# Batch 0 of an FFT-filtered gated FFN: both exchanges between transform stages moved from DRAM onto the chip

## The chip, the core and the metric

The kernel runs on one core of a Trainium2 chip. A core has five engines that work from queues of their own: TensorE (PE: matmuls; PEld: its weight loads), VectorE (DVE), ScalarE (ACT), GpSimd (POOL) and SyncE (SP, which only issues DMA transfers here). The metric is device time in microseconds (us), the median over runs. The profile is of one further execution.

## The reference

Eight sequences x of 3136 tokens by 256 channels are filtered along the tokens in the frequency domain, and then go through a gated feed-forward network with 1024 hidden channels.

```python
X = np.fft.rfft(x, axis=1)
Y = X * (filt_r + 1j * filt_i)[None]
x = np.fft.irfft(Y, n=3136, axis=1)
h = np.maximum(x @ w_in, 0.0)
conv_out = ...  # depthwise, 3 taps along the tokens, weights conv_w
out = (h * (1.0 / (1.0 + np.exp(-conv_out)))) @ w_out
```

Inputs x and filt are float32; w_in, conv_w and w_out arrive as float64 and are turned into float32 on the chip.

## The kernel before

**The transform.** 3136 is 112 times 28. One sequence goes through four matmul stages, each in 14 steps ("pairs" q, two of 28 columns each):

- Stage 1: for a pair of residues n, a matmul over 112 tokens gives 112 numbers (2 parts s, real and imaginary, 28 groups g) for 256 channels. `by_column` (L229) makes it with the table as the stationary operand: numbers on partitions, channels in the free dimension.
- Stage 2: for a pair of groups g, a matmul over (n, r), which is 28 times 4 rows, gives 56 bins in two layouts; `filt` (L240) multiplies by the filter on DVE (L244 to L246) and adds on POOL (L247).
- Stage 3: `by_column` again, with the inverse tables (in_i) and z from `filt`.
- Stage 4: `fourth` (L250): here the data is the stationary operand and a table the moving one, so the outcome has channels on partitions, as the network needs it. It is split into a rounded part (`hi_act` on ACT, L145) and a rest (`lo_dve` on DVE, L148), both called y.

Between stages 1 and 2, and between 3 and 4, the rows have to be regrouped: what lay on 112 partitions for one n is wanted as (n, r) rows for one g. Before the change this goes through DRAM: `store` (L224) copies PSUM to st on ACT (L226) and writes a_dram or b_dram, and loads (`load_in`, L219) read them back with another view.

**The order of the work.** Batch 0's transform and the weight conversion stand in a block of their own at the start (L262 to L388), written out by hand in the order of every engine's queue. After it comes the main loop (L575 on), in which the network of batch t-1 and the transform of batch t run together by a plan; its first matmuls over y (L176 to L178, tile ps_h) need all of batch 0's y for the first tokens, hence all 14 steps of stage 4.

The block before, in order: SP loads stage 1's tables (tab from in_s) and x (rows), the conv weights and the first weight chunks (raw); stage 1 runs and its stores go out on ACT's DMA queue; SP loads the filters (f), the inverse tables, and the rows of a_dram; stages 2 and 3 run interleaved, step i of stage 2 beside step i-3 of stage 3; four steps of batch 1's stage 1 follow (AHEAD); SP loads the rows of b_dram; stage 4 runs.

**The weight conversion.** `to_f32` (L153) turns one chunk of float64 into float32 with seven DVE instructions (L159 to L171) and one POOL add (L173); there are eight chunks of 128x512 and a small one ("c", the conv weights). `split_weights` (L289) splits a chunk into rounded part and rest: two ACT copies, two POOL subtractions. Chunk buffers (raw) are three, so the load of chunk k+3 waits for the conversion that held the buffer. Before, chunks c and 0 to 2 are converted ahead of stage 2, then 3 to 5, and 6 and 7 within stages 2 and 3.

**The filters.** f has four buffers. For each pair two DMAs load one half each into 64 partitions (L304, L305), and ACT copies them to the other 56 partitions (L309, L310).

Of the kernel before, what the change touches and what calls it, by code (L numbers as in the profile page):

```python
# [17 lines left out]
N1 = 112  # L18
# [20 lines left out]
def _dft_tables():  # L39
# [69 lines left out]
    return {"s1": s1, "s2": s2(False), "s2s": s2(True), "i1": i1, "m2": m2}  # L109
# [15 lines left out]
def tile_fft_filter_gated_ffn(  # L125
# [10 lines left out]
    s2s: bass.AP,  # L136
    i1: bass.AP,
# [54 lines left out]
    s2s_sb = wc.tile([112, 120], F32, name="s2s_sb")  # L192
    cw = wc.tile([128, 3, NF], F32, name="cw")
# [9 lines left out]
    yps = [ctx.enter_context(tc.tile_pool(name="y_even", bufs=1, side="right"))]  # L203
# [46 lines left out]
    def fourth(ps, br):  # L250

        for j in range(2):
            for k in range(KT):
                o = ps[:, (2 * k + j) * N1:(2 * k + j + 1) * N1]
                nc.tensor.matmul(o, lhsT=br[:, j, 128 * k:128 * k + 128], rhs=m2_sb, start=True, stop=True)  # L255
# [6 lines left out]
    with (  # L262
        tc.tile_pool(name="sp", bufs=2) as sp,
# [3 lines left out]
        raws, fts, tabs, rows, zs = {}, {}, {}, {}, {}  # L267

        def load_weights(k):
            raws[k] = raw = sp.tile([128, 2, 512], I32, name="raw", bufs=3)  # L270
            for part, src in enumerate((w_in, w_out)):
                nc.sync.dma_start(out=raw[:, part], in_=src[:, 512 * k:512 * k + 512])

        def load_conv():
            raws["c"] = raw = sp.tile([128, 2, 512], I32, name="raw", bufs=3)
            nc.sync.dma_start(out=raw[:, 0, 0:6 * NF], in_=conv_w)

        def convert(k):

            raw = raws.pop(k)  # L280
            em = sp.tile([128, 2, 512], I32, name="em")
# [3 lines left out]
            else:  # L285
                ws[k] = w = sp.tile([128, 2, 256], F32, name="ws", bufs=8)
                yield from to_f32(w.rearrange("p t n -> p (t n)"), raw.rearrange("p t n -> p (t n)"), em[:, 0], em[:, 1])

# [8 lines left out]
        def table(kind, c):  # L297
            k, src, n = {"1": (112, s1, 7), "3": (120, i1, 3)}[kind]
            tabs[kind, c] = t = sp.tile([120, 4, 112], F32, name=f"tab{kind}", bufs=n)[0:k]
            nc.sync.dma_start(out=t, in_=src[:, 4 * c:4 * c + 4])  # L300

        def load_filter(q):
            fts[q] = f = sp.tile([120, 2, 2, D], F32, name="f", bufs=4)
            nc.sync.dma_start(out=f[0:64, :, 0], in_=filt_in[0:64, pair(q), 0])  # L304
            nc.sync.dma_start(out=f[56:120, :, 1], in_=filt_in[56:120, pair(q), 1])  # L305

        def copy_filter(q):
            f = fts[q]
            nc.scalar.activation(f[64:120, :, 0], f[0:56, :, 0], AF.Copy)  # L309
            nc.scalar.activation(f[0:56, :, 1], f[64:120, :, 1], AF.Copy)  # L310
            if q == NP - 1:
                nc.scalar.dma_start(out=f[92:93, 1, 0], in_=nyq)

        def load(kind, b, q):
            rows[kind, q] = load_in(sp, kind, b, q, 12, "rows")

        def column_stage(kind, b, q, r):
            ps = sps.tile([128, 512], F32, name="ps")
            by_column(ps, tabs[kind, q // 2][:, 2 * (q % 2):2 * (q % 2) + 2], r)
            store(tp, kind, b, q, ps, 3, "st", nc.scalar)  # L320

        ws = {}
        for c in range(7):
            table("1", c)
            load("1", 0, 2 * c)
            load("1", 0, 2 * c + 1)
            if c == 0:
                load_conv()
            if c < 2:
                load_weights(c)  # L330
        for dst, src in ((s2_sb, s2[:, 0:120]), (s2s_sb, s2s[:, 0:120]), (m2_sb, m2)):
            nc.sync.dma_start(out=dst, in_=src)
        for k in ("c", 0, 1, 2):
            for _ in convert(k):
                pass
            load_weights(2 if k == "c" else k + 3)
        for q in range(NP):
            column_stage("1", 0, q, rows.pop(("1", q)))
        for q in range(4):
            load_filter(q)  # L340
        for c in range(2):
            table("3", c)
        for q in range(NP):
            load("2", 0, q)
        for k in (3, 4, 5):
            for _ in convert(k):
                pass
            if k + 3 < 8:
                load_weights(k + 3)
        table("3", 2)  # L350
        for q in range(4):
            copy_filter(q)
        late = (x for k in (6, 7) for x in convert(k))
        pss = {}
        for i in range(NP + 4):
            if i < NP:
                pss[i] = ps = sps.tile([128, 512], F32, name="ps")
                second(ps, i, rows.pop(("2", i)))
            if 0 <= i - 3 < NP:
                q = i - 3  # L360
                column_stage("3", 0, q, zs.pop(q))
                if q % 2 and q // 2 + 3 < 7:
                    table("3", q // 2 + 3)
            if 0 <= i - 1 < NP:
                zs[i - 1] = filt(pss.pop(i - 1), i - 1, fts.pop(i - 1))
# [289 lines left out]
```

## Time and profile before

| | |
|---|---|
| median of 3 runs | 1602.9 us (1602.11 to 1603.8) |
| the profiled execution, its own time | 1603.2 us |
| its span in the trace | 1601.4 us |
| mean granted TensorE clock | 0.982 |
| PE matmul busy | 1525.1 us (95%) |
| DVE, ACT, POOL busy | 1197.2, 1202.3, 874.8 us |
| DMA, mean over the span | 149 GB/s, 238.32 MB |
| first matmul that waits for batch 0's y | starts at 130.93 us |

The profile has one line for a group of instructions, with the source line, the engine, output and inputs by the program's names, the shape, the count, the busy time and the mean duration. A timeline line begins with the start and the duration in us; in brackets stands how long the engine had been idle and what ended that. "Issue" is waiting that no recorded event explains. An ordinary float32 matmul appears as two MATMUL records (the 56 matmuls of stage 4 are 112 records). "Granted clock" is the share of full speed that TensorE was allowed.

### The profile page before, as it was taken

The page shows a single profiled execution, that of the slowest core. Times are in us where ns is not written, and L with a number is a line of the kernel's source. Part 1 is how long each engine was busy: PE and PEld are TensorE (multiplying, and loading weights), DVE is VectorE, ACT ScalarE, POOL GpSimd, SP SyncE. Part 2 cuts the span into 40 slices and gives each one's busy share as a digit, 9 for nine tenths or more (in the row PEclk, how much of TensorE's full clock was granted, in tenths as well). Part 3 has the DMA queues.
Part 4 walks back from the last instruction along what each step waited for, and adds up shares of the span by engine and source line. Part 5 has one row for each costly group of instructions (what it writes and reads, how often), then busy time and mean ns, then how long its engine had stood idle before and what let it go on. Part 6 is the DMA issues. An engine that isn't in the chain of part 4 may idle for free.

```text
span 1601.4 us, 28391 instructions
## 1 busy us (share of the span) xinstructions
PE 1525.1 (95%) x9424; PEld 1366.8 (85%) x9424; DVE 1197.2 (75%) x1966; ACT 1202.3 (75%) x2623; POOL 874.8 (55%) x1170
## 2 busy tenths in 40 slices
PE   4569999999999999999999999999999999999999
PEld 3248889988899888998899987998889988899998
DVE  4856887578866787768876778767887788777876
ACT  2448667876699767986678866887669966799897
POOL 1452555655566455655556555565556755576554
PEclk8679999999999999999999999999999999999999
DMA  9876565465544665356553565546554445320001
GB/s 298 242 213 199 178 187 165 144 190 155 166 128 145 182 185 152 111 158 188 163 165 110 167 180 150 152 129 183 158 164 131 134 129 175 101 66 24 24 24 37
DMA packets 171874, 238.32 MB, mean 149 GB/s; under 512 B 16744, under 2 KB 119505, under 8 KB 171729
## 3 DMA queue, kind: packets, MB, share of 16 engines
q1 hardware_dynamic: 165615, 229.17, 48.1%
q10 hardware_dynamic: 6114, 7.34, 1.4%
q8 instruction: 75, 1.23, 0.3%
q14 instruction: 70, 0.57, 0.1%
HBM read 159.38 MB, written 77.07 MB: 148 GB/s over the span
## 4 chain that ended last, share of the span: by engine, by line
PE 62%; issue 14%; POOL 9%; DVE 6%; DMA 3%; ACT 3%; SPq 1%; POOLq 0%; ACTq 0%; DVEq 0%
PE po L459 8%; PE po L460 8%; PE po L461 8%; PE ps_h L176 8%; PE ps_h L177 8%; PE ps_h L178 8%; PE ps_t L231 7%; POOL g L151 6%; PE ps_t L255 5%; DVE t L423 2%; POOL gm L151 2%; PE ps_t L235 2%; ACT t L419 1%; POOL z L247 1%; DMA raw<-in_w_out 1%
## 5 line engine op out<-in xcount | busy, mean ns | idle before, releaser
L423 DVE SCALAR_TENSOR_TENSOR t<-ps_h,cw,t 128x448 f32<-128x448 f32 x896 | 608.0, 679 | 329.7 <-ACT t L419 324.9
L151 POOL TENSOR_TENSOR g<-t,g 128x384 fp32r<-128x384 f32 x448 | 455.2, 1016 | 200.8 <-ACT g L145 88.2
L419 ACT ACTIVATE t<-ps_h,cw 128x448 f32<-128x448 f32 x448 | 284.5, 635 | 241.2 <-POOL gm L151 209.1
L176 PE MATMUL ps_h<-y,wi 128*128 128x450 f32 x896 | 410.2, 458 | 0.0
L459 PE MATMUL po<-wo,g 128*128 128x256 f32 x1344 | 374.2, 278 | 0.5
L460 PE MATMUL po<-wo,g 128*128 128x256 f32 x1344 | 373.9, 278 | 0.0
L461 PE MATMUL po<-wo,g 128*128 128x256 f32 x1344 | 373.4, 278 | 0.0
L247 POOL TENSOR_TENSOR z<-z,v 120x512 f32<-120x512 f32 x112 | 145.2, 1296 | 348.5 <-DVE v L246 315.1
L177 PE MATMUL ps_h<-y,wi 128*128 128x450 f32 x896 | 328.8, 367 | 0.3 <-DVE y L148 0.3
L178 PE MATMUL ps_h<-y,wi 128*128 128x450 f32 x896 | 328.7, 367 | 0.0
L415 ACT ACTIVATE ps_h<-ps_h 128x450 f32<-128x450 f32 x448 | 243.6, 544 | 68.8 <-PE ps_h L178 67.5
L429 DVE TENSOR_TENSOR t<-ps_h,t 128x448 f32<-128x448 f32 x448 | 274.9, 614 | 0.6 <-ACT t L426 0.6
L459 PEld LDWEIGHTS po<-wo,g 128*128 128x128 f32 x1344 | 253.1, 188 | 7.0 <-DVE ot L474 3.1
L460 PEld LDWEIGHTS po<-wo,g 128*128 128x128 f32 x1344 | 252.4, 188 | 3.8
L426 ACT ACTIVATE t<-t 128x448 f32<-128x448 f32 x448 | 254.4, 568 | 0.9 <-DVE t L423 0.9
L461 PEld LDWEIGHTS po<-wo,g 128*128 128x128 f32 x1344 | 253.2, 188 | 0.0
L145 ACT ACTIVATE g<-t 128x384 fp32r<-128x384 f32 x448 | 229.8, 513 | 0.2 <-DVE t L429 0.2
L151 POOL TENSOR_TENSOR y<-z,y 128x448 fp32r<-128x448 f32 x98 | 138.1, 1411 | 121.9 <-ACT y L145 117.7
L176 PEld LDWEIGHTS ps_h<-y,wi 128*128 128x128 f32 x896 | 169.5, 189 | 37.4 <-issue 22.3
L177 PEld LDWEIGHTS ps_h<-y,wi 128*128 128x128 f32 x896 | 170.3, 190 | 35.0 <-issue 22.6
L178 PEld LDWEIGHTS ps_h<-y,wi 128*128 128x128 f32 x896 | 168.6, 188 | 15.4
L151 POOL TENSOR_TENSOR gm<-t,gm 128x64 fp32r<-128x64 f32 x448 | 145.2, 324 | 0.0
(72 smaller groups left out, 1923.3 us busy)
## 6 DMA issues: line engine op xcount, KB each, us to landing
filt<-in_filt SPq DMA_DIRECT2D x98, 512.0 KB, 5.3
tin<-a_dram SPq DMA_DIRECT2D x98, 224.0 KB, 4.3
b_dram<-st SPq DMA_DIRECT2D x98, 224.0 KB, 2.4
tin<-b_dram SPq DMA_DIRECT2D x98, 224.0 KB, 3.1
out<-ot SPq DMA_DIRECT2D x84, 256.0 KB, 2.2
tin<-in_x SPq DMA_DIRECT2D x94, 224.0 KB, 3.5
a_dram<-st SPq DMA_DIRECT2D x94, 224.0 KB, 2.4
tab<-in_i SPq DMA_DIRECT2D x98, 105.0 KB, 4.5
```

The costliest lines, as they stand in the source:

```text
L151: nc.gpsimd.tensor_tensor(out=dst, in0=src, in1=hi.bitcast(F32), op=ALU.subtract)
L176: nc.tensor.matmul(ps, lhsT=wh, rhs=rh, start=start, stop=False, **kw)
L177: nc.tensor.matmul(ps, lhsT=wh, rhs=rl, start=False, stop=False, **kw)
L178: nc.tensor.matmul(ps, lhsT=wl, rhs=rh, start=False, stop=stop, **kw)
L415: nc.scalar.activation(hs[u, f], hs[u, f], AF.Relu)
L419: nc.scalar.activation(t, hs[u, f][:, 1:SUB + 1], AF.Copy, scale=cw[:, 1, f:f + 1])
L423: nc.vector.scalar_tensor_tensor(out=t, in0=h[:, k:SUB + k], scalar=cw[:, k, f:f + 1], in1=t, op0=ALU.mult, op1=ALU.add)
L426: nc.scalar.activation(ts[u, f], ts[u, f], AF.Sigmoid)
L429: nc.vector.tensor_mul(ts[u, f], hs.pop((u, f))[:, 1:SUB + 1], ts[u, f])
L459: nc.tensor.matmul(o, lhsT=gh, rhs=wo[0][:, f], start=first, stop=False, skip_group_check=True)
L460: nc.tensor.matmul(o, lhsT=gh, rhs=wo[1][:, f], start=False, stop=False, skip_group_check=True)
L461: nc.tensor.matmul(o, lhsT=gl, rhs=wo[0][:, f], start=False, stop=last, skip_group_check=True)
```

## The change

Only the block for batch 0 changes; on every engine the queue of the main loop is the same as before, row for row.

- Stages 1 and 3 swap the operands (`turned_stage`): the data is stationary, the table moves, so the outcome has channels on partitions. A step is four matmuls (two columns j, two channel halves k) with 112 moving columns, where it was two with 256. ACT copies the outcome into one large tile that stays in SBUF: at for stage 1, bt for stage 3.
- The exchange is made by reading: `turn_back` takes 112 columns of at or bt for one g (or c), 28 elements apart, four times, and transposes each piece with TensorE against an identity matrix (one_sb) into a PSUM bank, which ACT copies to a tile ar or br of 112 partitions. Stages 2 and 4 then run on it as they did on the loaded rows. Stage 4 uses a table m2g with its rows in another order, and stage 3's table is read with a step of four elements.
- The stores to and the loads from a_dram and b_dram go for batch 0 (14 of each).
- A filter pair is now one DMA of 128 partitions that brings both halves, into three buffers; the ACT copies and the small nyq DMA go.
- The conversion becomes one sequence of steps (`csteps`) that is drawn on through the block: two steps beside each step of stage 1, one beside each of stages 2 and 3 and of the four of batch 1, two beside each of stage 4. `split_weights` follows one chunk behind.
- The y tiles of even batches come from a pool that is opened after the tiles of the first stages are given back.

```diff
+    one_sb = wc.tile([128, 128], F32, name="one_sb")
...
-    yps = [ctx.enter_context(tc.tile_pool(name="y_even", bufs=1, side="right"))]
+    yps = []
...
+        m2g = sc.tile([112, N1], F32, name="m2g", bufs=1)
+        bt = sc.tile([128, KT, G, 112], F32, name="bt", bufs=1)
...
+        def convert_all():
+            for k in range(8):
+                yield from convert(k)
+                if k + 3 < 8:
+                    load_weights(k + 3)
+                if k > 0:
+                    split_weights(k - 1)
+            split_weights(7)
...
-        def load_filter(q):
-            fts[q] = f = sp.tile([120, 2, 2, D], F32, name="f", bufs=4)
-            nc.sync.dma_start(out=f[0:64, :, 0], in_=filt_in[0:64, pair(q), 0])
-            nc.sync.dma_start(out=f[56:120, :, 1], in_=filt_in[56:120, pair(q), 1])
-        def copy_filter(q):
...
+        def turned_stage(r, tab):
+            ps = bank()
+            for j in range(2):
+                for k in range(KT):
+                    o = ps[:, (2 * k + j) * 112:(2 * k + j + 1) * 112]
+                    nc.tensor.matmul(o, lhsT=r[:, j, 128 * k:128 * k + 128], rhs=tab[j], start=True, stop=True)
+            return ps[:, 0:4 * 112].rearrange("p (k j m) -> p k j m", k=KT, j=2)
+        def turn_back(cols, pool, tag):
+            ps = bank()
+            for j in range(2):
+                for k in range(KT):
+                    nc.tensor.transpose(ps[0:112, j * D + 128 * k:j * D + 128 * k + 128], cols(j, k), one_sb)
+            r = pool.tile([112, 2, D], F32, name=tag, bufs=3)
+            nc.scalar.activation(r, ps[0:112].rearrange("p (j d) -> p j d", d=D), AF.Copy)
+            return r
...
-        for q in range(NP):
-            column_stage("1", 0, q, rows.pop(("1", q)))
...
-        for q in range(NP):
-            load("2", 0, q)
...
+            at = sq.tile([128, KT, N2, 112], F32, name="at", bufs=1)
...
+            def load_filter(q):
+                fts[q] = f = sq.tile([128, 2, 2, D], F32, name="f", bufs=3)
+                nc.sync.dma_start(out=f, in_=filt_in[:, pair(q)])
...
+            for q in range(NP):
+                ps = turned_stage(rows.pop(("1", q)), [tab("1", q)[:, j] for j in range(2)])
+                nc.scalar.activation(at[:, :, pair(q)], ps, AF.Copy)
+                conversion(2)
...
+            for i in range(NP + 4):
+                if i < NP:
+                    back = [at[:, k].rearrange("p n (r g) -> p (n r) g", g=G) for k in range(KT)]
+                    rows["2", i] = turn_back(lambda j, k: back[k][:, :, 2 * i + j], sq, "ar")
+                if 0 <= i - 1 < NP:
+                    pss[i - 1] = ps = bank()
+                    second(ps, i - 1, rows.pop(("2", i - 1)))
+                if 0 <= i - 4 < NP:
+                    q = i - 4
+                    ps = turned_stage(zs.pop(q), [tab("3", q)[:, j].rearrange("p (c r) -> p r c", r=4) for j in range(2)])
+                    nc.scalar.activation(bt[:, :, pair(q)], ps, AF.Copy)
...
+                if 0 <= i - 2 < NP:
+                    zs[i - 2] = filt(pss.pop(i - 2), i - 2, fts.pop(i - 2))
+                    if i + 1 < NP:
+                        load_filter(i + 1)
+                conversion(1)
...
-        for q in range(NP):
-            load("4", 0, q)
-        for q in range(NP):
-            ps = sps.tile([128, 512], F32, name="ps")
-            fourth(ps, rows.pop(("4", q)))
+        yps.append(ctx.enter_context(tc.tile_pool(name="y_even", bufs=1, side="right", reuse_waits="tile")))
+        for q in range(NP + 1):
+            if q < NP:
+                back = [bt[:, k].rearrange("p g (r c) -> p c (g r)", r=4) for k in range(KT)]
+                rows["4", q] = turn_back(lambda j, k: back[k][:, 2 * q + j], sc, "br")
+            if q:
+                ps = bank()
+                fourth(ps, rows.pop(("4", q - 1)), m2g)
...
+            conversion(2)
```

The order on SP behind batch 0's loads of x, up to the first filters. Before (tin is batch 1's x, raw a weight chunk, here chunk 5, f filters, tab_304 an inverse table; the four pairs of f rows are shown once):

```order
L221 DMA tin<-in_x 112x512 x3
L272 DMA raw<-in_w_in 128x512
L272 DMA raw<-in_w_out 128x512
L304 DMA f<-in_filt 64x2x256
L305 DMA f<-in_filt 64x2x256
...
L300 DMA tab_304<-in_i 120x448
L300 DMA tab_306<-in_i 120x448
L221 DMA rows<-a_dram_57 112x512 x14
```

With the change, at the same place (raw is again chunk 5; m2g is the reordered table of stage 4):

```order
L223 DMA tin<-in_x 112x512 x3
L276 DMA raw<-in_w_in 128x512
L276 DMA raw<-in_w_out 128x512
L344 DMA tab_313<-in_i 120x448
L344 DMA tab_315<-in_i 120x448
L351 DMA f<-in_filt 128x1024 x3
L344 DMA tab_323<-in_i 120x448
L379 DMA m_sb<-in_m 112x112
L381 DMA m2g<-in_m 28x112 x4
```

The 14 loads of a_dram are gone from SP's queue, and the first three filters stand behind chunk 5 and two inverse tables; chunk 5 waits for the buffer of chunk 2.

The order on DVE around the first filter product (tile z; L160 to L172 are the conversion's lines in the changed kernel, chunk 3 and the start of chunk 4):

```order
L168 SCALAR_TENSOR_TENSOR ws<-em 128x512
L170 TENSOR_SCALAR em<-ws 128x512
L172 SCALAR_TENSOR_TENSOR em<-raw,em 128x512
L160 TENSOR_SCALAR em<-raw 128x512
L162 TENSOR_SCALAR em<-raw 128x512
L246 TENSOR_TENSOR z<-ps,f 120x512
L247 TENSOR_TENSOR v_87<-ps,f 56x512
L248 SCALAR_TENSOR_TENSOR v_87<-ps,f 56x512
L164 TENSOR_TENSOR em<-em 128x512
```

Four chunks and two steps of the fifth stand ahead of the first filter product (before: c and chunks 0 to 5), and one conversion step stands between any two filter products.

The order on TensorE from the end of the four steps of batch 1 to the main loop. Before:

```order
L231 MATMUL ps<-rows,tab_104 112x256 x4
L231 MATMUL ps<-rows,tab_115 112x256 x4
L255 MATMUL ps<-m_sb,rows 128x112 x56
L231 MATMUL ps_t<-tin,tab 112x256 x4
L176 MATMUL ps_h<-y_741,wi_82 128x450
```

With the change (L327 are the transposes out of bt, L257 stage 4):

```order
L233 MATMUL ps<-rows,tab_108 112x256 x4
L233 MATMUL ps<-rows,tab_116 112x256 x4
L327 MATMUL ps<-one_sb,bt 112x128 x8
L257 MATMUL ps<-m2g,br 128x112 x4
L327 MATMUL ps<-one_sb,bt 112x128 x4
L257 MATMUL ps<-m2g,br 128x112 x4
```

Four transposes now stand between any two steps of stage 4, running one step ahead of it; after the last one come the same four matmuls on tin and the first over y.

More of the change, by code (lines that the diff above doesn't have):

```diff
@@ L108, in _dft_tables @@
     i1 = np.concatenate([i1[0], np.zeros((8, G, 112)), i1[1]])
[L109 removed]
+    return {"s1": s1, "s2": s2(False), "s2s": s2(True), "one": np.eye(128), "i1": i1, "m2": m2}
 def _bins():
@@ L136, in tile_fft_filter_gated_ffn @@
     s2s: bass.AP,
+    one: bass.AP,
     i1: bass.AP,
@@ L254, in fourth @@
                 o = ps[:, (2 * k + j) * N1:(2 * k + j + 1) * N1]
-                nc.tensor.matmul(o, lhsT=br[:, j, 128 * k:128 * k + 128], rhs=m2_sb, start=True, stop=True)
+                nc.tensor.matmul(o, lhsT=br[:, j, 128 * k:128 * k + 128], rhs=m, start=True, stop=True)
     def as_y(p):
@@ L266, in tile_fft_filter_gated_ffn @@
     ):
-        raws, fts, tabs, rows, zs = {}, {}, {}, {}, {}
+        raws, ws, fts, tabs, rows, zs, pss = {}, {}, {}, {}, {}, {}, {}
+        m2g = sc.tile([112, N1], F32, name="m2g", bufs=1)
+        bt = sc.tile([128, KT, G, 112], F32, name="bt", bufs=1)
         def load_weights(k):
-            raws[k] = raw = sp.tile([128, 2, 512], I32, name="raw", bufs=3)
+            raws[k] = raw = sc.tile([128, 2, 512], I32, name="raw", bufs=3)
             for part, src in enumerate((w_in, w_out)):
@@ L274, in load_conv @@
         def load_conv():
-            raws["c"] = raw = sp.tile([128, 2, 512], I32, name="raw", bufs=3)
+            raws["c"] = raw = sc.tile([128, 2, 512], I32, name="raw", bufs=3)
             nc.sync.dma_start(out=raw[:, 0, 0:6 * NF], in_=conv_w)
@@ L322, in tile_fft_filter_gated_ffn @@
[L322 to L334, printed above, removed]
-                pass
-            load_weights(2 if k == "c" else k + 3)
@@ L354, in tile_fft_filter_gated_ffn @@
[L354 to L365, printed above, removed]
-                if i + 3 < NP:
-                    load_filter(i + 3)
-            if 4 <= i + 2 < NP:
-                copy_filter(i + 2)
-            if i > 1:
-                next(late, None)
-            if 4 <= i < 12:
-                if i == 10:
-                    for _ in late:
-                        pass
-                split_weights(i - 4)
@@ L377, in tile_fft_filter_gated_ffn, with bank @@
-        for q in range(AHEAD):
-            load("1", 1, q)
-        for q in range(AHEAD):
-            column_stage("1", 1, q, rows.pop(("1", q)))
-        for q in range(NP):
-            load("4", 0, q)
-        for q in range(NP):
-            ps = sps.tile([128, 512], F32, name="ps")
-            fourth(ps, rows.pop(("4", q)))
-            yh, yl = y_slices(0, pair(q))
-            hi_act(yh, as_y(ps[:, 0:4 * N1]))
-            lo_dve(yl, as_y(ps[:, 0:4 * N1]), yh)
+        def bank():
+            return sps.tile([128, 512], F32, name="ps")
@@ L390, in tile_fft_filter_gated_ffn @@
+        for _ in csteps:
+            pass
     yps.append(ctx.enter_context(tc.tile_pool(name="y_odd", bufs=1, reuse_waits="tile")))
```

82 lines of the change are left out of this document (51 added, 31 removed).

## The prediction

> **What bounds the kernel now.** I read the busy time by stretches first (columns: stretch, its length, busy time and records of PE, PEld, DVE, ACT, POOL, then granted clock, DMA share, GB/s), cut where batch 0's block changes its stage: stage 1, the gap behind it, stages 2 and 3, batch 1's four steps and the gap behind them, stage 4.
>
> ```profile
> 0.00:33.00 33.00, 18.68 (x56) 12.46 (x56) 9.72 (x22) 9.84 (x16) 4.31 (x10) 0.91 0.92 287
> 33.00:48.50 15.50, 0.00 (x0) 0.00 (x0) 14.95 (x24) 5.02 (x8) 4.13 (x3) 0.50 0.91 284
> 48.50:105.00 56.50, 37.67 (x85) 20.07 (x86) 44.69 (x61) 24.97 (x49) 35.40 (x37) 0.74 0.78 221
> 105.00:112.50 7.50, 4.21 (x18) 3.05 (x16) 0.00 (x0) 2.98 (x5) 0.00 (x0) 0.95 0.70 200
> 112.50:131.00 18.50, 18.09 (x122) 17.30 (x122) 12.93 (x14) 13.92 (x16) 0.00 (x0) 0.82 0.67 173
> ```
>
> The first half is a DMA stage: share 0.92, and TensorE does nothing for 15.5 us, at a clock of 0.50, while DVE converts weights. Then the chain of waits, of which these are the pieces that carry the exchanges and the loads around them (start, length, what):
>
> ```profile
> 27.49 5.33 DMA raw<-in_w_out
> ...
> 43.76 3.97 DMA tab<-in_i
> ...
> 47.80 6.56 DMA rows<-a_dram
> 54.37 6.88 DMA raw<-in_w_out
> ...
> 106.38 2.23 DMA b_dram<-st
> 108.75 3.67 DMA rows<-b_dram
> 112.56 7.18 PE ps L255 x32
> ```
>
> Until 61 us the chain is DMA nearly throughout, with the reload of a_dram and the weight chunks queued around it; the second exchange shows with its store and its reload, 5.9 us. Then TensorE's and DVE's timelines fix the points between which the change works:
>
> ```profile
> 48.58 6.60 PE L235 MATMUL ps<-rows,s_sb 112*120 112x512 f32 x8 [20.29 <-issue]
> ...
> 56.89 1.12 PE L231 MATMUL ps<-z,tab 120*112 120x256 f32 x4
> 57.84 1.02 PE L235 MATMUL ps<-rows,s_sb 112*120 112x512 f32 x2
> ...
> 65.60 2.05 PE L231 MATMUL ps<-z,tab 120*112 120x256 f32 x4 [6.73 <-POOL z L247]
> ...
> 100.26 5.46 PE L231 MATMUL ps<-z,tab 120*112 120x256 f32 x12 [1.47 <-POOL z L247]
> 105.51 3.71 PE L231 MATMUL ps<-rows,tab 112*112 112x256 f32 x16
> 112.56 16.10 PE L255 MATMUL ps<-m_sb,rows 112*128 112x112 f32 x112 [3.34 <-DMA rows<-b_dram]
> ...
> 130.93 0.45 PE L177 MATMUL ps_h<-y,wi 128*128 128x450 f32 x1 [0.35 <-DVE y L148]
> ```
>
> ```profile
> 41.52 0.42 DVE L159 TENSOR_SCALAR em<-raw 128x512 int32<-128x512 int32 x1
> 41.86 1.49 DVE L161 TENSOR_SCALAR em<-raw 128x512 int32<-128x512 int32 x1
> ...
> 46.37 0.42 DVE L159 TENSOR_SCALAR em<-raw 128x512 int32<-128x512 int32 x1
> ...
> 51.20 0.68 DVE L244 TENSOR_TENSOR z<-ps,f 120x512 f32<-120x512 f32 x1
> ...
> 64.45 0.69 DVE L244 TENSOR_TENSOR z<-ps,f 120x512 f32<-120x512 f32 x1
> ...
> 67.34 0.69 DVE L244 TENSOR_TENSOR z<-ps,f 120x512 f32<-120x512 f32 x1
> ...
> 100.95 0.69 DVE L246 SCALAR_TENSOR_TENSOR v<-ps,f 56x512 f32<-56x512 f32 x1
> ```
>
> So the filter products run from 51.20 to 101.64, stage 4 from 112.56 to 128.66, and the first matmul that waits for y starts at 130.93, 2.27 us behind stage 4. The main loop's queues are not changed, so I take the rest of the span, 1601.4 - 130.9 = 1470.5 us, as it is, and forecast when that matmul starts. The other durations come from the groups of this stretch and its DMA issues (KB each, median us to landing):
>
> ```profile
> L247 POOL TENSOR_TENSOR z<-z,v 120x512 f32<-120x512 f32 x14 | 19.6, 1406 | 10.5 <-DVE v L246 10.5
> ...
> L226 ACT ACTIVATE st<-ps 112x512 f32<-112x512 f32 x32 | 18.9, 591 | 30.4 <-PE ps L231 23.6 <-DMA a_dram<-st 5.9 <-DMA b_dram<-st 0.5
> ...
> L145 ACT ACTIVATE y<-ps 128x448 fp32r<-128x448 f32 x14 | 12.9, 1005 | 6.2 <-PE ps L255 6.2
> ...
> L310 ACT ACTIVATE f<-f 56x512 f32<-56x512 f32 x14 | 8.8, 628 | 0.3
> ...
> L145 ACT ACTIVATE wi<-ws 128x256 fp32r<-128x256 f32 x8 | 3.3, 417 | 0.4 <-POOL ws L173 0.2
> ```
>
> ```profile
> rows<-in_x SPq DMA_DIRECT2D x18, 224.0 KB, 5.2
> ...
> f<-in_filt SPq DMA_DIRECT2D x28, 128.0 KB, 3.6
> rows<-a_dram SPq DMA_DIRECT2D x14, 224.0 KB, 6.5
> ...
> raw<-in_w_in SPq DMA_DIRECT2D x8, 256.0 KB, 5.9
> ...
> tab<-in_i SPq DMA_DIRECT2D x7, 210.0 KB, 3.8
> tab<-in_s SPq DMA_DIRECT2D x7, 196.0 KB, 4.7
> ...
> filt<-in_filt SPq DMA_DIRECT2D x1, 512.0 KB, 5.5
> ```
>
> **Stage 1 and the first filter product.** Up to the last x, SP issues 7 tables of 196 KB, 14 rows of 224, two chunks of 2 x 256 and 0.2 MB of small tables: 5.9 MB. At the 287 GB/s of the first stretch that is 20.4 us, so x is in at about 22. Each of the swapped steps has the shape of stage 4's matmuls, whose 112 records took 16.10 us: 0.144 each, 1.15 a step, and an ACT copy like L226 without the store. That follows the loads, and stage 1 ends near 23.5. The stores that shared the DMA engines are gone; counting their bandwidth as the reads' is an estimate.
>
> DVE decides next, because four chunks and two steps stand ahead of its first product. Chunk 2 is the first load behind x: 0.5 MB more, in at 23. Chunks 2 and 3 take 4.85 us each (41.52 to 46.37), and the two steps of chunk 4 0.42 and 1.49: 23 + 9.7 + 1.9 = 34.6. The filter comes at the same time: chunk 5, ahead of it on SP, waits for chunk 2's conversion at 27.9; then 0.5 MB of chunk, two tables and the first filter are 1.48 MB, 5.2 us at that rate, and issue and landing bring it to 34 or so. Stage 2's first steps lie in between, in TensorE's idle time. I take 34.5, against 51.20: **16.7 us earlier**.
>
> **Fourteen products.** A step of three products and one conversion step of 0.69 took 2.89 us (64.45 to 67.34); some conversion steps take 1.49 instead. The filters now come as 512 KB into three buffers: a buffer is free again after 0.6 us of issue, 5.5 of landing and 2.2 of products, 8.3 us for three steps, 2.8 each. DVE's and the loads' paces are so close that neither absorbs the other's delays; I take 3.2, so 44.8 us, ending at 79.3. Before it was 50.4: **5.6 us more**. The stall of 6.88 us for chunk 6 goes, since the chunks come well ahead. TensorE needs per step the transposes, 1.02 and 1.15, and ACT 0.59 for ar, about as much for bt and a share of 0.4 a copy: below 3.2 both. ACT's filter copies, 28 of 0.63, go at no gain, being beside DVE.
>
> The price of four transposes is not in the trace. From below: one record each, at stage 4's pace, is 4 x 0.144 = 0.57. From above: two records each as an ordinary float32 matmul, 128 columns for 112, is 8 x 0.144 x 128/112 = 1.31; a stretch of their weight loads by the step of 28 elements stays within that, if it is like the one of ACT's writes to y with that step (1005 ns, where the contiguous st, a seventh larger, takes 591): 0.57 x 1.9 = 1.1. It cannot be less than nothing, as these instructions are added; at nothing the end would come 8 us sooner, but 128 columns have to be loaded and streamed each time, as in those rows. I take 0.57, the row of the nearest shape, and keep 1.31. The Trainium skill, page "TensorE: Matmul & The Clock Gate", section "Part 4: PE-mode transpose", gives about 275 ns for a transpose within a kernel; by it four take 1.1 us, and the forecast below would be some 8 us later. No run here shows it yet.
>
> **From the last product to stage 4.** POOL adds (1.4), stage 3's last step runs (1.15), then batch 1's four steps (3.7): 79.3 + 6.3 = 85.6. Before, the same took from 101.64 to 109.2, 7.6: **1.3 gained**. Then two steps of transposes (1.1), ACT's two copies of a chunk (0.8) and one of br (0.6): 88.1. That is 2.5 in place of the 3.34 that waited for b_dram: **0.8 gained**. The conversion of chunk 7 stands in this stretch, too; ACT waits for its POOL add a microsecond at most, and TensorE has banks to run ahead.
>
> **Stage 4.** Per step TensorE has 1.15 + 0.57 = 1.7 us, ACT 0.6 + 1.0 = 1.6, DVE 1.0: TensorE sets the pace, 14 x 1.7 = 23.8 instead of 16.1: **7.7 lost**, ending at 111.9. With the same 2.27 behind it, the first waiting matmul starts at 114.2.
>
> **The sum.** 16.7 + 5.6 + 1.3 + 0.8 - 7.7 = 16.7 us earlier. The profiled execution took 1603.2, 0.3 over the median of 1602.9; 1603.2 - 16.7 - 0.3 gives 1586 us. Fewer DMA bytes after that point (no rest of b_dram to read) are worth nothing, as TensorE works through there.
>
> **Rivals.**
>
> *The products keep a slower pace.* Stages 2 and 3 must now move 14 x 512 KB of filters, four tables, two chunks and batch 1's first x, some 10.6 MB in 45 us, 235 GB/s, where that stretch had 221 at a share of 0.78; a reload in a full queue took 6.5 us to land. With 8 us to land a step is (8 + 0.6 + 2.2) / 3 = 3.6, 5.6 us in all; transposes of 1.31 bring a TensorE step to 3.5 and stage 4 to 14 x 2.46, 10.5 us more. The two together give 1602, either one 1592 to 1597. For it: three buffers for four. Against: one large DMA of 512 KB landed in 5.5 us, not four times the 3.6 of 128 KB. Chance 0.25.
>
> *TensorE stays at half clock through the transposes.* The clock was 0.50 after the idle 15.5 us, and 0.74 in stages 2 and 3, where PE was busy 37.67 of 56.5. At half clock four records of stage 3 took 2.05 instead of 1.12. If that holds in stage 4's loop, a step is 3.4 and the loop 47.6: 7 us slower than before, 1610; if in stages 2 and 3 as well, a step there is 5.5 and the end near 1642. It decides from 2.9 us per step of stage 4 (1.7 + 16.7/14). Against it: from 48.58, eight cold records in 6.60 us were enough for the 1.12 at 56.89, and two thirds of the new loop are ordinary matmuls. Chance 0.1. The page named above says, in that section, that transposes do not count as activity for the clock; if they count as idle, this rival is what it predicts, and the trace, without a transpose, bears on it only through those two thirds.
>
> *The exchanges were covered anyway.* DVE's conversions fill the 15.5 us gap (14.95 busy), and their sum is not reduced; if chunk 2 still lands at 32.8 as before, the first product comes at 44 and only 7 of the 16.7 us remain: with the rest of the sum 1596, and with transposes of 1.31 as well, no change. Against it: chunk 2 was late through 14 stores ahead of it. Chance 0.07, of which 0.05 faster and 0.02 within the bound below.
>
> **How the numbers follow.** The forecast, 1578 to 1592, has 0.55; more gain than that, by loads that land some us sooner and steps of 2.9, 0.03. About 0.2% (3.2 us) is what a measurement of this kernel tells from no change. Of the slower pace, 0.20 falls under 1599.7, 0.04 within the bound and 0.01 above it. Faster: 0.55 + 0.03 + 0.20 + 0.05 = 0.83; same 0.04 + 0.02 = 0.06; slower 0.10 + 0.01 = 0.11. The range runs from 1577 (products at 2.9 and 5 us less for the loads) to 1601 (transposes of 1.31 or slow filter loads); half clock lies outside.
>
> **What would show it.** In the changed profile: the first L246 product near 34.5, the last near 79; the mean step between 3.0 and 3.5; transposes (L327) as 56 or 112 records per exchange, 0.14 us apart; the granted clock above 0.8 in stage 4's loop; first matmul on y at 114. I am wrong in the step concerned if DVE waits for f in more than a few steps, if the loop of stage 4 takes over 30 us, or if the rest of the span is not 1470 us.

## The result, and the profile after

| | before | after |
|---|---|---|
| median | 1602.51 us (4 runs, 1600.54 to 1603.8) | 1592.85 us (4 runs, 1592.42 to 1593.62) |
| the profiled execution, own time / span | 1603.2 / 1601.4 us | 1592.42 / 1590.6 us |
| first matmul that waits for y | 130.93 us | 121.34 us |
| span behind it | 1470.5 us | 1469.3 us |

The ratio is 0.9941, 95% interval 0.9924 to 0.9959: 9.7 us faster, where 16.5 were forecast. The part of the span that was to stay as it was did so within 1.2 us, so all that is to be explained lies ahead of 121.34.

The busy times of after in the same stretches as before (length, then busy time and records of PE, PEld, DVE, ACT, POOL, granted clock, DMA share, GB/s):

```profile
0.00:33.00 33.00, 22.27 (x127) 20.48 (x128) 15.15 (x32) 12.40 (x25) 8.31 (x15) 0.90 0.94 263
33.00:48.50 15.50, 9.39 (x36) 6.52 (x36) 13.28 (x20) 2.55 (x5) 8.49 (x7) 0.78 0.83 266
48.50:105.00 56.50, 46.14 (x222) 39.61 (x220) 39.93 (x58) 21.52 (x41) 27.08 (x26) 0.85 0.56 162
105.00:112.50 7.50, 6.53 (x58) 6.53 (x59) 4.39 (x5) 7.50 (x13) 2.43 (x4) 1.00 0.00 0
112.50:131.00 18.50, 18.04 (x111) 15.79 (x110) 11.74 (x15) 15.91 (x29) 1.15 (x2) 1.00 0.49 143
```

TensorE's 15.5 us without work are gone, and from 105 us on it runs at full clock, with no DMA until 112.5. But the first stretch is still a DMA stage, at a share of 0.94, and its total rate fell from 287 to 263 GB/s. Before, 6.77 MB of that stretch were loads on SP's queue and 2.71 MB stores on ACT's, 205 and 82 GB/s; now all of it is loads. So the loads gained 58 GB/s of the 82 that the stores had, and not the whole.

DVE's timeline (start, length, what; in brackets the idle time before it and what ended that): chunk 2's first conversion step, the first filter product, the longest wait for a filter, the last product.

```profile
26.16 0.43 DVE L160 TENSOR_SCALAR em<-raw 128x512 int32<-128x512 int32 x1 [5.33 <-DMA raw<-in_w_out]
...
38.62 0.69 DVE L246 TENSOR_TENSOR z<-ps,f 120x512 f32<-120x512 f32 x1 [1.18 <-DMA f<-in_filt]
...
73.31 0.69 DVE L246 TENSOR_TENSOR z<-ps,f 120x512 f32<-120x512 f32 x1 [2.73 <-DMA f<-in_filt]
...
80.17 0.69 DVE L248 SCALAR_TENSOR_TENSOR v<-ps,f 56x512 f32<-56x512 f32 x1
```

And the sum of these waits for the filter (us in total, times, longest):

```profile
DVE z L246 <- DMA f<-in_filt: 6.0, 5, 2.7
```

The products run from 38.62 to 80.86, 42.2 us. What follows on TensorE, from the last step of stage 3 to the first matmul that waits for y:

```profile
84.53 2.05 PE L319 MATMUL ps<-tab,z 120*128 120x112 f32 x8 [2.60 <-POOL z L249]
86.40 4.65 PE L233 MATMUL ps<-rows,tab 112*112 112x256 f32 x16
90.89 1.04 PE L327 MATMUL ps<-one_sb,bt 128*112 128x128 f32 x8
95.61 2.05 PE L257 MATMUL ps<-m2g,br 112*128 112x112 f32 x8 [3.68 <-ACT br L329]
...
98.30 1.89 PE L257 MATMUL ps<-m2g,br 112*128 112x112 f32 x8
...
102.79 1.04 PE L257 MATMUL ps<-m2g,br 112*128 112x112 f32 x8
103.67 0.60 PE L327 MATMUL ps<-one_sb,bt 128*112 128x128 f32 x4
105.97 1.15 PE L257 MATMUL ps<-m2g,br 112*128 112x112 f32 x8 [1.70 <-ACT br L329]
...
107.39 1.04 PE L257 MATMUL ps<-m2g,br 112*128 112x112 f32 x8
108.27 0.60 PE L327 MATMUL ps<-one_sb,bt 128*112 128x128 f32 x4
108.71 1.09 PE L257 MATMUL ps<-m2g,br 112*128 112x112 f32 x8
...
121.34 0.44 PE L178 MATMUL ps_h<-y,wi 128*128 128x450 f32 x1 [0.27 <-DVE y L149]
```

A set of four transposes is four records, and from its start to that of the next matmul 0.44 us pass (108.27 to 108.71): 0.11 each. A warm step (one at full clock) of stage 4 takes 1.32 us (107.39 to 108.71). Two breaks stand against that: the wait of 3.68 us at 95.61, after which the records are slow for three steps (2.05, 1.89 and 1.68 instead of 1.04 to 1.15), and the wait of 1.70 at 105.97. POOL's and ACT's timelines show what is behind the waits at 84.53, 95.61 and 105.97:

```profile
79.80 1.27 POOL L174 TENSOR_TENSOR ws<-ws,em 128x512 f32<-128x512 f32 x1
81.04 0.91 POOL L152 TENSOR_TENSOR wi<-ws,wi 128x256 fp32r<-128x256 f32 x1
81.91 1.17 POOL L152 TENSOR_TENSOR wo<-ws,wo 128x256 fp32r<-128x256 f32 x1
83.04 1.44 POOL L249 TENSOR_TENSOR z<-z,v 120x512 f32<-120x512 f32 x1
```

```profile
93.36 0.60 ACT L228 ACTIVATE st<-ps 112x512 f32<-112x512 f32 x1 [2.42 <-DMA a_dram<-st]
...
94.35 0.42 ACT L146 ACTIVATE wi<-ws 128x256 fp32r<-128x256 f32 x1 [0.39 <-ACT st L228]
94.67 0.40 ACT L146 ACTIVATE wo<-ws 128x256 fp32r<-128x256 f32 x1
94.98 1.06 ACT L329 ACTIVATE br<-ps 112x512 f32<-112x512 f32 x2
...
104.71 0.42 ACT L146 ACTIVATE wi<-ws 128x256 fp32r<-128x256 f32 x1 [0.62 <-POOL ws L174]
```

The last product ends at 80.86, but POOL still has three operations of a weight chunk ahead of its last add. ACT stands 2.42 us for a free store buffer of batch 1's fourth step, then makes a chunk's two copies, and only then br. And in stage 4's loop the copies of chunks 6 and 7 come ahead of the next br, and those of chunk 7 wait for POOL's add of that chunk.

Against the prediction, in us:

| step | forecast | measured | difference |
|---|---|---|---|
| first product starts | 34.5 | 38.62 | +4.1 |
| fourteen products | 44.8 | 42.2 | -2.6 |
| last product to the end of batch 1's steps (91.05) | 6.3 | 10.2 | +3.9 |
| to stage 4's first matmul | 2.5 | 4.6 | +2.1 |
| stage 4's loop, 95.61 to 118.97 | 23.8 | 23.4 | -0.4 |
| to the first waiting y matmul | 2.27 | 2.37 | +0.1 |
| together | 114.2 | 121.34 | +7.2 |

### The profile page after: what moved, and what is told of

The parts are those of the page before. It is cut to its first block, busy times and chain, and to the rows that moved or that the text cites. A ratio compares the mean times of both kernels' runs of the same rounds, so it can differ in the third digit from the quotient of the medians.

```text
span 1590.6 us, 28686 instructions
## 1 busy us (share of the span) xinstructions
PE 1539.5 (97%) x9648; PEld 1395.2 (88%) x9648; DVE 1195.3 (75%) x1966; ACT 1197.6 (75%) x2623; POOL 877.1 (55%) x1170
## 4 chain that ended last, share of the span: by engine, by line
PE 62%; issue 15%; POOL 10%; DVE 5%; DMA 4%; ACT 3%; SPq 0%; POOLq 0%; ACTq 0%; DVEq 0%
PE po L492 8%; PE po L493 8%; PE po L494 8%; PE ps_h L177 8%; PE ps_h L178 8%; PE ps_h L179 8%; POOL g L152 7%; PE ps_t L233 6%; PE ps_t L257 5%; DVE t L456 2%; POOL gm L152 2%; PE ps_t L237 2%; DMA f<-in_filt 1%; DMA rows<-in_x 1%; ACT t L452 1%
```

## The experiments

| kernel | median, us | ratio to before | interval |
|---|---|---|---|
| the change | 1592.85 | 0.9941 | 0.9924 to 0.9959 |
| first exchange only | 1590.52 | 0.9929 | 0.9912 to 0.9946 |
| second exchange only | 1609.66 | 1.0052 | 1.0037 to 1.0067 |
| both through DRAM, the other edits kept | 1608.12 | 1.0044 | 1.0029 to 1.0059 |
| three filter pairs loaded | 1590.14 | 0.9932 | 0.9918 to 0.9947 |
| batch 1's steps early | 1588.41 | 0.9912 | 0.9897 to 0.9927 |
| table turned | 1592.88 | 0.994 | 0.9925 to 0.9955 |
| no conversion in stage 3's tail | 1592.67 | 0.9939 | 0.9924 to 0.9954 |
| these three and four filter buffers together | 1584.33 | 0.9888 | 0.9871 to 0.9904 |
| chunk 7's copies later | 1589.66 | 0.9925 | 0.9912 to 0.9937 |
| together, and chunk 7's copies later | 1577.57 | 0.9852 | 0.9838 to 0.9865 |
| stage 4's transposes doubled | 1592.41 | 0.9944 | 0.9932 to 0.9957 |
| second exchange through DRAM, with the late copies | 1589.0 | 0.9922 | 0.9908 to 0.9935 |

### Which exchange is worth how much

**The first exchange alone.** The second goes through DRAM again.

```diff
-    ps = turned_stage(zs.pop(q), ...)
-    nc.scalar.activation(bt[:, :, pair(q)], ps, AF.Copy)
+    ps = bank()
+    by_column(ps, tab("3", q), zs.pop(q))
+    store(tp, "3", 0, q, ps, 3, "st", nc.scalar)
...
+for q in range(NP):
+    rows["4", q] = load_in(sc, "4", 0, q, 12, "rows4")
```

> First exchange on chip, second one back through DRAM (stage 3 by column with stores to b_dram, 14 loads back, stage 4 on the loaded rows). Theory A, mine: the second exchange on chip costs more than the round trip that it replaces, because the loop of stage 4 takes 23.4 us in place of 16.1 and waits for ACT's copies; then the first matmul over y starts near 111 us instead of 121.3, and the time is about 1582 to 1585 us. Rival B: the round trip (store, reload of 3.2 MB) hides nothing of itself and stands in full behind the last step of stage 3; then the matmul starts at 124 or later and the time is 1595 to 1600 us.

Neither range held it. Stage 4 takes 14 us again (97.11 to 111.2) instead of 23.4, but then TensorE stands and starts at half speed, as its row shows:

```profile
116.30 2.05 PE L233 MATMUL ps_t<-tin,tab 112*112 112x256 f32 x4 [4.11 <-DVE y L149]
```

The first matmul over y comes at 117.78. DVE makes y in 0.9 us a step, and is late because the change has put conversion into this loop: DVE has four steps of it between the first y, and then waits 2.13 us for ACT, which stands 2.64 us for POOL's add of chunk 7 (104.72). With a faster stage 4, y becomes the bound.

**The second exchange alone.** Stage 1 stores to a_dram, stage 2 loads from it.

```diff
-    ps = turned_stage(rows.pop(("1", q)), ...)
-    nc.scalar.activation(at[:, :, pair(q)], ps, AF.Copy)
+    ps = bank()
+    by_column(ps, tab("1", q), rows.pop(("1", q)))
+    store(tp, "1", 0, q, ps, 3, "st", nc.scalar)
...
+for q in range(NP):
+    rows["2", q] = load_in(sq, "2", 0, q, 14, "rows2")
```

> Second exchange on chip, first one through DRAM (stage 1 by column with stores to a_dram, 14 loads back), the rest as in the change. Theory A: the gain belongs to the first exchange, so this is no faster than before, 1601 to 1610 us, with the first filter product back near 48 to 52 us. Rival B (the gain comes from the new order of the weight conversion and the single filter load): 1590 to 1596 us.

TensorE waits for the reload again, and the first product starts at 52.58:

```profile
50.51 5.89 PE L237 MATMUL ps<-rows,s_sb 112*120 112x512 f32 x8 [20.74 <-DMA rows<-a_dram]
```

**Neither.** Both edits above; what stays of the change is the new order of the conversion, the single filter DMA into three buffers and the late y tiles.

> Both exchanges through DRAM, but with the change's conversion order, its single filter load and its three filter buffers. Theory A: within 4 us of before, 1598 to 1606 us; then the exchanges on chip are what gains, and together with the two runs that keep one of them this gives the worth of each. Rival B: the other edits gain by themselves, 1590 to 1596 us.

These other edits alone cost 6.5 us over the same job's 1601.66. Their profiled execution, the fastest of the four, shows 3.7 us of it: stage 4 starts at 112.30, as before (112.56), but the first matmul over y only at 134.63 (before: 130.93). Chunk 7's conversion stands in this loop: ACT waits 2.73 us for POOL's add of it (119.91) before it goes on with y, DVE's last y comes late behind that, and TensorE waits for it and is slow afterwards. Of DVE and of TensorE:

```profile
121.56 9.82 DVE L149 TENSOR_TENSOR y<-ps,y 128x448 fp32r<-128x448 f32 x11 [2.12 <-ACT y L146]
```

```profile
131.44 3.75 PE L233 MATMUL ps_t<-tin,tab 112*112 112x256 f32 x8 [5.40 <-DVE y L149]
```

With the change itself the four kernels make a square. The first exchange on chip is worth 17.6 us beside a second one through DRAM (1608.12 to 1590.52) and 16.8 beside one on chip (1609.66 to 1592.85): the whole gain, and more than it. The second makes 1.5 to 2.3 us of loss, with intervals that overlap, so that a loss is not settled either; a gain does not show. The prediction had the second at 0.8 - 7.7, a loss of 6.9: it is smaller, since in these kernels the wait for y takes most of what a faster stage 4 saves.

### What holds the products

**Three filter pairs only.** The first three pairs are loaded and used again for the rest, so the filter of the later bins is left out; everything else is as in the change (fs holds the first three).

```diff
 if i + 1 < NP:
-    load_filter(i + 1)
+    fts[i + 1] = fs[(i + 1) % 3]
```

> The change, but only the first three filter pairs are loaded and used again and again (leaves out the other eleven pairs, so later bins get wrong filter values). Theory A: the filter loads set the pace of the products: DVE's 6.0 us of waiting for f go, the products end 5 to 6 us sooner, time 1586 to 1588 us. Rival B: TensorE sets the pace, 2.92 us a step with no idle record between 47 and 73 us, since stage 3's matmuls take 0.20 a record with the table read in steps of four: products no more than 2 us shorter, 1590.5 to 1592.5 us.

The products take 38.3 us (39.21 to 77.54) instead of 42.2, and the time falls by 2.7 us by the medians (1.4 by the ratios, whose intervals overlap): between the two expectations. So the waits of 6.0 us for f cost 1 to 3 us of time, not 6. What holds the products without them is two paces at once: DVE waits only 1.0 us for the first f and 0.7 us for TensorE in all that time, and TensorE's steps follow each other every 2.92 us without a gap (50.58 to 73.49).

**The table turned.** Stage 3's moving operand was read with a step of four elements; here the table is stored in the order in which it is read.

```diff
-    turned_stage(zs.pop(q), [tab("3", q)[:, j].rearrange("p (c r) -> p r c", r=4) for j in range(2)])
+    turned_stage(zs.pop(q), [tab("3", q)[:, j] for j in range(2)])
```

> The change, with stage 3's table stored in the order in which it is read, so that the moving operand is contiguous (one more table from the host; the main loop keeps the old one). Theory A: the read in steps of four elements costs 0.07 us a record, 0.20 against the 0.13 of stage 1's same shape, and TensorE's pace of 2.92 us sets the products; records fall to 0.11 to 0.13, products end 1 to 3 us sooner, limited by the filter loads, 1590 to 1592 us. Rival B: the records stay at 0.20, since it is the 120 rows of z or the clock, and nothing moves: 1592 to 1593.5 us.

Stage 3's step on TensorE falls from 1.60 us, from its start to that of the next instruction (58.72 to 60.32 in the change), to 0.87 (65.72 to 66.59). The change's row, and then this kernel's:

```profile
58.72 1.78 PE L319 MATMUL ps<-tab,z 120*128 120x112 f32 x8
```

```profile
65.72 1.04 PE L320 MATMUL ps<-tab,z 120*128 120x112 f32 x8
```

That is 0.11 a record instead of 0.20, at full clock in both (granted 0.99 in the change from 47 to 72 us, 1.00 here from 61 to 67). The products still take 41.4 us, and the time is the same. DVE waits 3.8 us in them, which the profile puts down to TensorE's ps and not to f; what holds them here is open, and only that the table's step did not hold the time is shown.

### What holds the way from the last product to y

**Batch 1's steps early.** The four steps stand beside stage 3's last four instead of behind them.

```diff
+    if i >= NP:
+        ps = bank()
+        by_column(ps, tab("1", i - NP), rows.pop(("1", i - NP)))
+        store(tp, "1", 1, i - NP, ps, 3, "st", nc.scalar)
...
-for q in range(AHEAD):
-    ...
+conversion(AHEAD)
```

> The change, with batch 1's four steps of stage 1 moved up: one each ahead of stage 3's last four steps, where TensorE waits 6 us for POOL, in place of all four behind them. Theory A: these steps (4.65 us on TensorE) and ACT's wait for the third store's buffer (2.4 us) stand on the path between the last step of stage 3 and stage 4; stage 4 starts 5 to 7 us sooner, near 89 to 90 us, and the time is 1586 to 1588 us. Rival B: the time there belongs to the two copies of br behind ACT's chunk copies, and what is saved is lost again in the first steps of stage 4: 1591 to 1593 us.

Stage 4 starts at 89.57, 6.0 us sooner, and 4.2 us of that reach y (117.18), because one wait in the loop grows:

```profile
99.20 2.05 PE L257 MATMUL ps<-m2g,br 112*128 112x112 f32 x8 [3.35 <-ACT br L329]
```

**No conversion steps beside stage 3's last four**, so that POOL's last z has nothing ahead of it.

```diff
-    conversion(1)
+    if i < NP:
+        conversion(1)
```

> The change, without conversion steps in the last four iterations of stages 2 and 3 (they come later, beside stage 4). Theory A: POOL's last z waits behind the add and the two subtractions of a weight chunk; without them it is done 2 us sooner and so is all that follows: 1590 to 1591.5 us. Rival B: the four steps are paid in stage 4, where ACT waits for POOL's add of the last chunk: 1592 to 1594 us.

POOL's last z now starts at 80.00 instead of 83.04 and stage 4 at 91.79 instead of 95.61; all of it is lost again in the loop, where the conversion now comes. TensorE's and ACT's rows:

```profile
106.16 2.05 PE L257 MATMUL ps<-m2g,br 112*128 112x112 f32 x8 [4.50 <-ACT br L329]
```

```profile
104.90 0.42 ACT L146 ACTIVATE wi<-ws 128x256 fp32r<-128x256 f32 x1 [3.42 <-POOL ws L174]
```

**These together**, with four filter buffers (and ten for x instead of twelve) and stage 4's tables loaded later.

```diff
-    f = sq.tile([128, 2, 2, D], F32, name="f", bufs=3)
+    f = sq.tile([128, 2, 2, D], F32, name="f", bufs=4)
```

> The three edits together, and four filter buffers instead of three (for ten x buffers instead of twelve) with stage 4's tables loaded later. Theory A: the terms add: 5 to 7 us for batch 1's steps, 2 for POOL, 2 to 4 for filters and the table: 1580 to 1585 us, the first matmul over y near 110 us. Rival B: each uncovers the next wait, and ACT, fully busy in stage 4, gives the last half back: 1586 to 1590 us.

8.5 us under the change, with stage 4 from 82.52. Batch 1's steps alone had 4.4 of that; how the rest divides among the other edits was not measured. The same wait shows once more:

```profile
97.37 2.05 PE L258 MATMUL ps<-m2g,br 112*128 112x112 f32 x8 [4.43 <-ACT br L330]
```

**Chunk 7's copies later.** If it is ACT standing on POOL's add of chunk 7, the copies only have to be drawn later.

```diff
                 if k > 0:
                     split_weights(k - 1)
+            for _ in range(4):
+                yield
             split_weights(7)
```

On the change itself:

> The changed kernel, with the copies of the last weight chunk (7) drawn two steps of stage 4 later, so that ACT does not stand on POOL's add of that chunk in front of the next br copy. Theory A: of stage 4's 23.4 us about 3 are that wait and the cold step behind it (1.7 us of waiting at 105.97, 0.9 for the records at half clock); the loop takes 20 to 21 us, the first waiting y matmul starts near 118.5, and the time is 1589 to 1591. Rival B: TensorE is held there by something else (the banks, or DVE's y behind it), the loop stays at 23 us and the time at 1592.5 to 1594.

In this kernel the lines behind the edit stand two further down (L331 is the change's L329). ACT's copies of chunks 6 and 7 start without a wait, and br follows at once; TensorE keeps its pace:

```profile
99.93 0.43 ACT L146 ACTIVATE wi<-ws 128x256 fp32r<-128x256 f32 x1
...
103.17 0.46 ACT L146 ACTIVATE wi<-ws 128x256 fp32r<-128x256 f32 x1
103.51 0.43 ACT L146 ACTIVATE wo<-ws 128x256 fp32r<-128x256 f32 x1
103.81 0.61 ACT L331 ACTIVATE br<-ps 112x512 f32<-112x512 f32 x1
```

```profile
95.28 1.15 PE L257 MATMUL ps<-m2g,br 112*128 112x112 f32 x8 [1.58 <-ACT br L331]
...
104.47 1.15 PE L257 MATMUL ps<-m2g,br 112*128 112x112 f32 x8 [0.35 <-ACT br L331]
...
117.16 0.44 PE L177 MATMUL ps_h<-y,wi 128*128 128x450 f32 x1 [0.48 <-DVE y L149]
```

The loop takes 19.5 us, y starts at 117.16, and the median is 3.2 us lower (2.6 by the ratios, whose intervals overlap). That fits theory A, but not all of it is the edit's: in this profile the wait ahead of the loop was 1.58 us and not 3.68, and the first three steps, which had cost the change some 3 us, were at full speed. What the edit is worth here is not settled. On the kernel with everything together:

> The kernel with all the edits together (batch 1's steps early, contiguous table, no conversion steps at stage 3's end, four filter buffers), and chunk 7's copies two steps later. Theory A: the stall of 4.43 us in stage 4's loop is ACT standing on POOL's add of chunk 7; without it the loop from 82.5 takes about 21 us, the first waiting y matmul starts near 106.5, and the time is 1578 to 1581. Rival B: the stall moves to another wait of the same length (DVE's y, or its conversion steps), 1583 to 1585.

```profile
78.61 1.15 PE L322 MATMUL ps<-tab,z 120*128 120x112 f32 x8 [2.36 <-POOL z L250]
...
82.19 1.86 PE L258 MATMUL ps<-m2g,br 112*128 112x112 f32 x8
...
96.21 1.15 PE L258 MATMUL ps<-m2g,br 112*128 112x112 f32 x8 [1.20 <-ACT br L332]
...
106.23 0.44 PE L179 MATMUL ps_h<-y,wi 128*128 128x450 f32 x1 [0.28 <-DVE y L150]
```

The longest wait in the loop is 1.20 us, where it was 4.43, and the time falls another 6.8 us (5.8 by the ratios, whose intervals do not overlap), to 1577.57: 15 us under the change, 1.5% under the kernel before. This settles that ACT's stand at POOL's add held the loop. It is the best version of the study, by the interval too.

### The price of the transposes, and the second exchange once more

**Stage 4's transposes doubled**: each set is written twice into the same bank.

```diff
-    for j in range(2):
+    for j in list(range(2)) * times:
```

> The changed kernel with each set of four transposes in stage 4 written twice into the same bank, 56 transposes more, same output. Theory A: a transpose costs TensorE 0.11 us, so a warm step of the loop takes 0.44 us more where TensorE paces it, and nothing where ACT does: 2 to 6 us longer, 1595 to 1599, with the granted clock still 1.00 from 105 us on. Rival B: transposes do not keep the clock up; with half of the records transposes it falls towards half in the loop, the steps go to 2.5 us or more, and the time is over 1605. By 275 ns a transpose, which the Trainium skill gives (page TensorE: Matmul & The Clock Gate, section Part 4: PE-mode transpose), the loop would be 15 us longer, 1608.

TensorE's timeline, and its clock in the loop's stretch (the column ahead of the last two):

```profile
97.07 1.04 PE L257 MATMUL ps<-m2g,br 112*128 112x112 f32 x8
97.95 1.04 PE L327 MATMUL ps<-one_sb,bt 128*112 128x128 f32 x8
98.82 1.04 PE L257 MATMUL ps<-m2g,br 112*128 112x112 f32 x8
```

```profile
95.00:120.00 25.00, 23.17 (x207) 22.93 (x208) 14.05 (x16) 20.57 (x31) 5.04 (x11) 1.00 0.02 5
```

A step now takes 1.75 us (97.07 to 98.82) instead of 1.32: 0.43 for four transposes, 0.11 each, and the clock stays at 1.00 with half of the records transposes. The Trainium skill, page "TensorE: Matmul & The Clock Gate", section "Part 4: PE-mode transpose", has about 275 ns a transpose and says that the full clock doesn't engage for them. As the duration of one record the trace agrees (272 ns in the change, 107 to 112.5 us), but as a price it does not: the next one starts after 0.11. On the clock the trace does not agree for transposes among ordinary matmuls; for transposes alone no run shows it.

The time itself did not rise (1592.41 against 1592.85, where theory A had 1595 to 1599). In the profile, 12 of the 14 added sets stand in the loop and cost it 5 us, and the other two stand ahead of it. The wait ahead of the loop was 0.71 us in this profile, and behind it the first steps ran at full speed, where the change lost some 3 us. So the loop took 24.9 us instead of 23.4, and y started at 122.52, 1.2 us later than in the change.

**The second exchange through DRAM, with the late copies, four filter buffers and no conversion in stage 3's tail.**

> The second exchange back through DRAM, with four filter buffers, no conversion steps at stage 3's end and chunk 7's copies two steps later; batch 1's steps stay behind stage 3. Theory A: with its stalls gone the second exchange on chip is worth what its store and reload took, 2 to 4 us, so this kernel stays behind the kernel with all edits together: 1583 to 1588. Rival B: the transposes cost stage 4 more than the store and reload did, since batch 1's steps cover these: 1577 to 1581, ahead of it.

1589.0, 11.4 us behind the kernel with everything together. Three rows show what is against it: the DMA stretch of stages 2 and 3, a wait that it makes, and the wait for y.

```profile
48.50:87.00 38.50, 25.41 (x99) 15.78 (x98) 30.53 (x45) 12.33 (x22) 20.62 (x16) 0.84 0.89 277
```

```profile
82.27 2.05 PE L233 MATMUL ps<-z,tab 120*112 120x256 f32 x4 [7.26 <-POOL z L249]
...
113.55 3.75 PE L233 MATMUL ps_t<-tin,tab 112*112 112x256 f32 x8 [3.77 <-DVE y L149]
```

With the stores to b_dram in the queue the share is 0.89 there (0.74 in the kernel with everything together), DVE waits 8.1 us for filters instead of 2.4, and its last product comes 6.3 us later (81.16 against 74.85 for its first instruction). Rival B falls. The two kernels also differ in where batch 1's steps stand and in the turned table, so the 11.4 us are not the exchange's alone; that the second exchange can pay is shown no further than that.

## Why the prediction was right or wrong

**Right: what the gain is and where it ends.** The first exchange carries it (17 us in the square), and the rest of the span stayed at 1469 us: 1469.3 in the change, 1469.2 with doubled transposes, 1469.4 in the best kernel. The forecast of 1586 was 6.9 us low, inside the range; the mechanism held and sizes were off. The time lies just above the likeliest stretch, 1578 to 1592, where the rival of slower products stood, though that rival did not come. And part of the nearness is luck: by the square the other edits cost 6.5 us, which the sum did not have, and the second exchange 1.5 to 2.3, where the sum had 6.9.

**The first product, 16.7 forecast, 12.6 measured.** The step "counting their bandwidth as the reads'" failed in size: the loads got 263 GB/s (205 before) and not 287. Chunk 2 was in at 26.16 and not 23; 0.8 us of that is a slip in the sum, as 0.5 MB at 287 GB/s behind an x at 22 gives 23.8. The conversion behind it, 11.6 us by the forecast, took 11.3, to 37.44; the filter, in the same queue, came last, 1.18 us later. That both would arrive together was right.

**The products, 3.2 us each, were 3.0.** Their bound was named rightly as two paces so close that neither absorbs the other: removing the waits for f (three filters) brought at most 2.7 us, and removing TensorE's longer step (the table turned) nothing. What wasn't counted is that stage 3's moving table has a step: 1.60 us a step for the 1.15 taken.

**From the last product to stage 4, 8.8 forecast, 14.8 measured: the largest miss.** "POOL adds (1.4)" took the row's duration and not its queue: 2.2 us of a chunk's operations stood ahead. The steps behind it were priced at full clock, though TensorE waits there for every z (granted clock 0.50 from 80 to 84.5 us, 0.69 from there to 91): 1.87 and 4.65 instead of 1.15 and 3.7, where 0.45 of the first difference is the table's step again. And the two copies of a chunk and one of br that the sum had for ACT left out the wait for a store buffer, 2.42.

**Stage 4, 23.8 forecast, 23.4 measured: right by two errors.** The transposes were too dear (0.57 a set, 0.44 measured) and so were the other records: the 0.144 of before came from a stretch at a clock of 0.82, at 1.00 it is 0.11. The warm step of 1.32 is TensorE's own, twelve records of 0.11 one behind the other, as forecast: doubling the transposes lengthens it by their full 0.43. ACT is as slow, busy 7.50 of 7.50 us from 105 to 112.5; its two copies of 0.66 and 1.0 overlap. Fourteen such steps are 18.5. The other 5 us are the three slow steps (7.2 us for 4.0) and the wait at 105.97 (3.2 for 1.3). "ACT waits for its POOL add a microsecond at most" was kept to the letter, with 0.62 us; what failed was taking it at nothing because "TensorE has banks to run ahead": with the copies of two chunks around it that wait delays br, and TensorE stands 1.70 us. As soon as the loop starts sooner, ACT's wait grows to 2.3 to 3.4 us and TensorE's to 3.35 to 4.50, as three experiments show.

**The rivals.** The slower pace of products did not come (3.0, not 3.6). The half clock did not come from transposes: in stage 4's loop of the change the clock is low only behind the wait of 3.68, and it is 1.00 there with doubled transposes. The change's stretch:

```profile
95.00:105.00 10.00, 8.67 (x48) 8.47 (x48) 5.03 (x7) 5.83 (x11) 3.01 (x8) 0.66 0.07 20
```
That the exchanges were covered anyway falls with the square. A cost that no rival had is that of the other edits, 6.5 us when alone: chunk 7's conversion in stage 4's loop holds back y, and by the profile that is 3.7 of them.

## What to carry to other kernels

A transfer taken off a critical path is worth what the next queues leave: write down, for each engine in the stretch behind it, what stands ahead of the instruction that the path needs, and move that first; here the late order of two copies decided about 6 us (0.9888 to 0.9852). An edit that wins nothing alone (the table, the conversion steps) may only have laid bare the next wait; try it again once that wait is gone. What these two added to the best kernel was not measured by itself. Take a matmul's duration from a stretch at full clock, and then ask whether the new stretch has the waits that lose it.

## What the runs showed of the hardware

- A moving operand read with a step of four float32 elements cost 0.20 us a record of 112 columns, a contiguous one 0.11, both at full clock. The Trainium skill, page "Advanced Engine Details and Errata", section "Memory Cachelines", has 16-byte lines in SBUF and a penalty when each access is in another; a step of 16 bytes is that case, and the trace agrees. The stationary operand of the transposes, read with a step of 28 elements, showed no such cost: 0.11 a transpose, and its weight loads took 179 ns (median, 107 to 112.5 us in the change).
- Waits of TensorE cost it its clock, and not always at once. In stage 4's loop it stayed at full speed behind waits of 1.20 to 1.70 us (1.15 for the eight records, and the next steps as fast), and was at half speed at once behind 3.35 to 4.50 us (2.05). In between the loss came later: behind 2.36 us (78.61 in the best kernel) the eight records took 1.15 at a clock of 0.97, but behind a further 0.64 us, from 80.40 to 84.00, the clock was 0.54, and the step at 82.19 took 1.86; behind 2.35 us (101.28 with three filters) it was 1.00 for 1.4 us and then 0.56 until 106.5. The Trainium skill, page "TensorE: Matmul & The Clock Gate", section "Why this matters for your kernels", puts the limit at about 3 us; the trace agrees for the longer waits, but not for these two.
- Taking the stores out of a full DMA stretch gave the loads most of their bandwidth, not all: 205 GB/s of loads beside 82 of stores, 263 of loads without them, at shares of 0.92 and 0.94.
